# Four early weight halves held back until the last pair's scores, two loads begun ahead of the layers, two halves a step in the first block

## The chip, the cores and the metric

The kernel runs on one core of one Trainium2 chip. The metric is the device time of one launch in microseconds (us). Before the change three runs took 1002.86, 1002.90 and 1004.34 us, with a median of 1002.9 us.

## The reference

Inputs are q, k and v of shape (4, 8, 576, 64) and four weight matrices in fp32. What is computed, cut to its core:

```python
scores = scale * q @ k.T                       # per batch and head, 576 x 576
mask = block_i >= block_j                      # causal by blocks of 64
attn = exp(scores - max); attn = attn / (sum + 1e-9)
x = (attn @ v)                                 # -> 2304 tokens x 512
h = x @ w_in;  g = relu(h) ** 2;  x = g @ w_out      # layer 0, hidden width 2048
h = x @ w_in2; g = h * cos(h);    out = g @ w_out2   # layer 1
```

## The kernel before

**Attention.** Two heads of one batch form a pair, so there are 16 pairs. A pair has nine query blocks of 64. For each block i, TensorE (PE) multiplies the stacked queries of both heads with the keys up to block i (`scores`, L374). VectorE (DVE) takes the negated maximum (`nmax`, L386), ScalarE (ACT) the exponential with its sum (L391). GpSimd (POOL) adds the guard to the sums (L416), VectorE inverts them (`rinv`, L422) and GpSimd scales the probabilities P (L431). TensorE transposes P in 128 x 128 pieces, four to a PSUM bank, 25 to a pair (L452). ScalarE writes the high part of each bank (`PTh`, L457) and VectorE subtracts it for the low part (`PTl`, L460; the last, of 64 keys, is written into PTh). TensorE multiplies both parts with the split values `vhl` (L517), ScalarE moves one half of the result (`half`, L528) and VectorE joins the halves into `xall` (L531).

**The order in attention.** A planner (class `Plan`) sets it. Each operation is added with an engine, an estimated cost and a rank, which is a number of the table RANK plus ten times the pair. The planner gives each engine, again and again, the operation that can start first; among those that can start equally early the smallest rank wins. The result is one fixed list for each engine, which the chip runs in that order.

**The weights.** Each layer has 16 chunks of its hidden width, and each chunk has two weight halves, one of w_in (h = 0) and one of w_out (h = 1), 128 x 512 numbers stored as 64-bit words. A half is loaded (`raw`, L202, four buffers) and turned into a high and a low fp32r part by ten instructions: on VectorE `shift` (L205), `mask` (L212), `join` (L223), `sign` (L235), `power` (L241) and `low` (L265); on ScalarE `rebias` (L218) and `fraction` (L229); and `high`, which is on GpSimd (L259) while attention runs and on ScalarE (L256) in the layers. The halves are taken in the order in which the first block of tokens needs them: halves 0, 1 and 2 are w_in of chunks 0 to 2, half 3 is w_out of chunk 0, half 4 is w_in of chunk 3, then alternately w_out and w_in, up to half 28, which is w_in of chunk 15, and the last three of w_out. Layer 0 has halves 0 to 31.

EARLY halves, six of them, are put into the plan of attention. All others are turned by `convert()`, which the layers call. One call finishes the half that the call before it had begun, begins the next, and loads one more.

**The layers.** Tokens go through in blocks, 512 in the first. A step is one chunk of one block: `hidden` (12 matmuls, L614) makes h, ScalarE and VectorE make g and split it (`gs`: relu, square and the high part on ScalarE, the low part on VectorE, L629), and `output` (12 matmuls, L678) follows three steps later (LAG). The vector work of a chunk is issued one and two steps after its `hidden`. A table PACE says how many calls of `convert` follow each step: 1.67 in the first block, 2 in blocks that it does not name. When the last chunk of a block has been issued, the block after it is split into high and low parts (`Cut`: `xs`, L315 on ScalarE and L318 on VectorE), and the first `hidden` of the new block reads them. Halves of layer 1 wait until layer 0's buffers come free, in the last block of layer 0. Each engine runs its instructions in the order in which this code issues them. The first token block lies in batch 0, which pairs 0 to 3 make, so its `Cut` (four on ScalarE, four on VectorE) is part of the plan of attention.

Of the kernel before, what the change touches and what calls it, by code (L numbers as in the profile page):

```python
# [24 lines left out]


RANK = {
    "load": -165.7,
    "k scale": -157.7,
    "scores": 2.2,  # L30
    "maximum": -10.7,
    "exponential": -2.3,
    "guard": -163.0,
    "invert": -9.5,
    "scale": 29.9,
    "turn": 15.2,
    "turned high": -300.7,
    "turned low": 10.0,
    "value load": -108.7,
    "value high": 42.3,  # L40
    "value low": 41.1,
    "weighted": 21.0,
    "move": 20.5,
    "join": 18.3,
    "keep": 215.5,
    "add": 497.7,
    "zeros": -334.9,
    "weights": 136.7,
    "cut": 1000000.0,
}  # L50

# [79 lines left out]
def tile_block_causal_attention__then__two_ffn(  # L131
# [13 lines left out]
    NPAIR, _, S = kT.shape  # L145
    D = vp.shape[4]
# [23 lines left out]
    nc.vector.memset(new_bias, -7.0 * 2.0**30)  # L170

    WARM = 15
    EARLY = 6
    NA = 5
    w_a = ctx.enter_context(tc.tile_pool(name="w_a", bufs=NA))
    xs_p = ctx.enter_context(tc.tile_pool(name="xs", bufs=1))
# [8 lines left out]
    weights = {}  # L185
    LAG = 3
    loads = [((layer, c), h) for layer in range(2) for c in range(KF) for h in range(2)]
    loads.sort(key=lambda x: (x[0][0], x[0][1] + LAG * x[1], -x[1]))
    loads.reverse()
    loaded, begun = [], []  # L190
# [81 lines left out]
    def flush():  # L272
        while later:
            later.pop()()

    def convert():

        old = new = None
        flush()
        if begun:  # L280
            (layer, c), h = begun[0].key, begun[0].h
            if layer == 1 and c >= freed[h]:
                return
            old = begun.pop()
            old.sign()
        if loaded:
            new = loaded.pop()
            begun.append(new)
            new.shift()
        if old:  # L290
            old.power()
            old.high()
        if new:
            new.mask()
            new.rebias()
        if old:
            old.low()
        if new:
            new.join()
            later.append(new.fraction)  # L300
        if loads:
            loaded.append(Half(*loads.pop()))
            loaded[0].load()

    class Cut:

# [18 lines left out]
    def attention():  # L325
        with ExitStack() as actx:
            ap = actx.enter_context(tc.tile_pool(name="ap", bufs=1))
            ps = actx.enter_context(tc.tile_pool(name="ps", bufs=1, space=PSUM))
            plan = Plan([ps.tile([128, 512], F32, name=f"ps{r}") for r in range(6)])
# [170 lines left out]
            def add_weighted(p, e, i0, i1):  # L500

                rank = 10 * p + e + i0 / 20
                b, hp = divmod(p, KD)
                mine, other = slice(e * D, (e + 1) * D), slice((1 - e) * D, (2 - e) * D)
                pt = [t.rearrange("p (s e d) -> p s e d", e=2, d=D) for t in PT]
                todo = [
                    (j, max(i0, 2 * j), x)
                    for j in range(NCH)
                    if 2 * j < i1
                    for x in range(1 if j == NCH - 1 else 2)  # L510
                ]
                w, at = (i1 - i0) * D, slice(i0 * D, i1 * D)

                def product(bank):
                    for n, (j, a, x) in enumerate(todo):
                        s0 = j_off[j] + a - 2 * j
                        nc.tensor.matmul(  # L517
                            bank[:, (a - i0) * D : w],
                            lhsT=vhl[:, j, e].rearrange("p x d -> p (x d)"),
                            rhs=pt[x][:, s0 : s0 + i1 - a, e, :],  # L520
                            start=(n == 0),
                            stop=(n == len(todo) - 1),
                        )

                x = xall[mine, hp, b * S : (b + 1) * S][:, at]

                def move(bank):
                    nc.scalar.activation(out=half[e][mine, at], in_=bank[other, 0:w], func=AF.Copy)  # L528

                def join(bank):  # L530
                    nc.vector.tensor_tensor(out=x, in0=bank[mine, 0:w], in1=half[e][mine, at], op=ALU.add)  # L531

                need = sorted({n // 4 for n, (_, i) in enumerate(seq) if i0 <= i < i1})
                keys = [f"{x}{g}" for x in ("PTh", "PTl", "room") for g in need] + ["vh", "vl"]
                cost = sum(max(0.107, (i1 - a) * D / 2400 + 0.0135) for _, a, _ in todo)
                s = plan.add("P", cost, ("weighted", rank), product, keys, [f"O{p}.{e}.{i0}"], holds=1)
                product_, half_, x_ = f"O{p}.{e}.{i0}", f"half{e}.{i0}", f"x{b}.{hp}.{e}.{i0}"
                out_of = lambda f: lambda bank=None: f(plan.held[s][0])
                plan.add("A", 0.052 + w / 1200, ("move", rank), out_of(move), [product_], [half_])
                plan.add("V", 0.07 + w / 960, ("join", rank), join, [product_, half_], [x_], frees=s)  # L540

            def add_zeros(r):

# [7 lines left out]
            def add_half(n):  # L551
                x = Half(*loads.pop())
                raw, high, bits = f"raw{n % 4}", f"high{n % 4}", f"bits{n % 2}"
                rank = ("weights", n)
                plan.add("D", 2.0, rank, x.load, writes=[raw, high])
                plan.add("V", 0.34, rank, x.shift, writes=[raw])
                plan.add("V", 0.34, rank, x.mask, [high], [bits])
                plan.add("A", 0.61, rank, x.rebias, writes=[bits])
                plan.add("V", 0.6, rank, x.join, [high], [raw])
                plan.add("A", 0.52, rank, x.fraction, writes=[raw])  # L560
                plan.add("V", 0.6, rank, x.sign, [high], [bits])
                plan.add("V", 0.34, rank, x.power, [bits], [high])
                plan.add("G", 0.67, rank, x.high_beside, [bits])
                plan.add("V", 0.6, rank, x.low, [raw, high])
# [5 lines left out]
            for p in range(NPAIR):  # L570
                if p < 2:
                    add_zeros(p)
                add_loads(p)
                for i in range(NB):
                    add_scores(p, i)
                for g in range(len(groups)):
                    add_normalise(p, g)
                for g in range((len(seq) + 3) // 4):
                    add_transposes(p, g)
                add_values(p)  # L580
                for e in range(2):
                    for i0, i1 in ((0, 4), (4, NB)):
                        add_weighted(p, e, i0, i1)
            for n in range(EARLY):
                add_half(n)
            for kk in range(KD):
                x = Cut(0, S // 128 * 128, kk)
                keys = [f"x0.{kk}.{e}.{i0}" for e in range(2) for i0 in (0, 4)]
                plan.add("A", 0.52, ("cut", kk), x.high, keys, [f"xs{kk}"])
                plan.add("V", 0.6, ("cut", kk), x.low, [f"xs{kk}"])  # L590
                first.append(x)
# [3 lines left out]
    def layers():  # L595
# [112 lines left out]
                t0 += n  # L708
        last = max(i for i, b in enumerate(blocks) if b[0] == 0)
        steps = [(i, c) for i in range(len(blocks)) for c in range(KF)]  # L710
        PACE = {0: 1.67, last: 1.75, last + 1: 0.75}
        owed = 0.0
        gss = {}
        xs = first
# [1 line left out]
        for step in range(len(steps) + LAG):  # L716
# [4 lines left out]
            if step < len(steps):  # L721
                i, c = steps[step]
                layer, t0, n = blocks[i]
                while (layer, c, 0) not in weights:
                    convert()
                gss[step], *fresh = hidden(layer, c, xs, n)
# [10 lines left out]
            if step < len(steps) and i == last:  # L737
                freed[0] = c + 1
            owed += PACE.get(i, 2)
            while owed >= 1:  # L740
                owed -= 1
                convert()
            if step >= LAG:
                i, c = steps[step - LAG]
                layer, t0, n = blocks[i]
                while (layer, c, 1) not in weights:
                    convert()
                output(layer, gss.pop(step - LAG), n, c)
                if i == last:
                    freed[1] = c + 1  # L750
                if c == KF - 1:
                    finish(layer, t0, n)

    with tc.manual_schedule():
        attention()
        layers()
# [43 lines left out]
```

## Time and profile before

| | us |
|---|---|
| median of three runs | 1002.9 |
| time of the profiled execution | 1003.09 |
| its span, first to last instruction | 1001.3 |
| TensorE busy | 981.8 (98%) |
| VectorE busy | 644.4 (64%) |
| ScalarE busy | 580.5 (58%) |
| GpSimd busy | 146.1 (15%) |
| first matmul of the layers starts | 202.96 |

TensorE is nearly always busy when the whole span is taken together. That is an average over stages: GpSimd works in attention alone (up to about 200 us), and VectorE is nearly full in attention and in the first block of layer 0 (up to about 282 us), while TensorE runs without a gap after that. The granted TensorE clock of the whole run was 0.998 of 2.4 GHz.

### The profile page before, as it was taken

What the parts mean: (1) busy time and instruction counts of PE and PEld (TensorE: products, weight loads), DVE (VectorE), ACT (ScalarE), POOL (GpSimd) and SP (SyncE); (2) the same over time, 40 slices, a digit from 0 to 9 for tenths busy, and PEclk for the clock granted to TensorE, in tenths of its full rate; (3) what the DMA queues carried; (4) which work ended last, traced back from release to release, by engine and by line L of the source; (5) the groups of instructions that cost most, each with busy time, mean ns of one, the idle gap of its engine ahead of it and who ended that gap; (6) DMA issues with size and microseconds to landing.
All of it is one profiled execution on the core that took longest, in us unless ns stands there. A gap on an engine that the chain in (4) does not pass through costs nothing.

```text
span 1001.3 us, 13718 instructions
## 1 busy us (share of the span) xinstructions
PE 981.8 (98%) x4895; PEld 823.2 (82%) x4895; DVE 644.4 (64%) x1292; ACT 580.5 (58%) x1192; POOL 146.1 (15%) x260
## 2 busy tenths in 40 slices
PE   8899999999999999999999999999999999999998
PEld 7677777888778889988888888888888888899996
DVE  5999999889972121211169999966555655656554
ACT  6898888878874343443368886644334434434433
POOL 6577777700000000000000000000000000000000
PEclk9999999999999999999999999999999999999999
DMA  6442332225430000000014442001000100100000
GB/s 224 139 141 98 98 99 99 98 87 169 166 125 1 1 1 1 1 1 1 1 63 139 163 141 85 1 1 42 1 1 1 43 1 1 43 1 1 32 1 31
DMA packets 18803, 58.54 MB, mean 58 GB/s; under 512 B 1968, under 2 KB 2096, under 8 KB 18736
## 3 DMA queue, kind: packets, MB, share of 16 engines
q1 hardware_dynamic: 18736, 57.68, 17.1%
q8 instruction: 38, 0.62, 0.3%
q14 instruction: 29, 0.24, 0.1%
HBM read 52.95 MB, written 4.72 MB: 58 GB/s over the span
## 4 chain that ended last, share of the span: by engine, by line
PE 78%; DVE 17%; ACT 2%; issue 1%; DMA 1%; POOLq 0%; POOL 0%; SPq 0%; ACTq 0%; DVEq 0%
PE acc L678 36%; PE h L614 36%; DVE nmax L386 3%; DVE PTl L460 3%; PE ps L374 2%; PE ps L517 2%; DVE w L265 2%; DVE raw L223 2%; DVE xall L531 2%; DVE bits L235 2%; PE ps L452 2%; DVE raw L205 1%; DVE raw L241 1%; DVE gs L629 1%; ACT P L391 1%
## 5 line engine op out<-in xcount | busy, mean ns | idle before, releaser
L614 PE MATMUL h<-xs,w 128*128 128x512 f32 (+2 forms) x1920 | 422.1, 369 | 1.8 <-ACT w L256 1.3
L614 PEld LDWEIGHTS h<-xs,w 128*128 128x128 f32 x1920 | 344.1, 188 | 59.6 <-ACT w L256 3.4
L678 PE MATMUL acc<-gs,w 128*128 128x512 f32 (+1 forms) x960 | 210.2, 368 | 0.0
L678 PE MATMUL acc<-w,gs 128*128 128x512 f32 x864 | 209.7, 391 | 0.0
L678 PEld LDWEIGHTS acc<-gs,w 128*128 128x128 f32 x960 | 168.4, 189 | 29.9
L629 DVE TENSOR_TENSOR gs<-g,gs 128x512 fp32r<-128x512 f32 (+2 forms) x160 | 101.4, 634 | 141.6 <-ACT gs L626 141.5
L678 PEld LDWEIGHTS acc<-w,gs 128*128 128x128 f32 x864 | 161.8, 188 | 32.1
L626 ACT CAST gs<-g 128x512 fp32r<-128x512 f32 (+2 forms) x160 | 92.3, 577 | 150.0 <-DVE g L661 96.7
L647 DVE SCALAR_TENSOR_TENSOR g<-turns,h 128x512 f32<-128x512 int32 (+1 forms) x80 | 50.7, 634 | 123.0 <-ACT turns L644 122.2
L374 PE MATMUL ps<-kB,qB 128*128 128x64 f32 (+7 forms) x256 | 83.9, 427 | 4.4 <-DVE PTl L460 1.6
L644 ACT ACTIVATE turns<-h 128x512 int32<-128x512 f32 (+1 forms) x80 | 44.2, 552 | 70.5 <-PE h L614 70.4
L636 ACT ACTIVATE g<-h 128x512 f32<-128x512 f32 (+1 forms) x80 | 43.8, 548 | 66.7 <-PE h L614 65.9
L431 POOL TENSOR_SCALAR P<-P,rinv 128x64 f32<-128x64 f32 (+2 forms) x144 | 78.0, 556 | 29.0 <-DVE rinv L422 27.0
L391 ACT ACTIVATE P<-ps,nmax 128x64 f32<-128x64 f32 (+7 forms) x128 | 64.1, 503 | 24.1 <-DVE nmax L386 19.4
L658 ACT ACTIVATE g<-g,half_pi 128x512 f32<-128x512 f32 (+1 forms) x80 | 54.6, 682 | 36.9 <-DVE g L652 36.9
L452 PEld LDWEIGHTS ps<-ident,P 128*128 128x128 f32 (+1 forms) x400 | 47.3, 141 | 34.4 <-DVE PTl L460 14.0
L452 PE MATMUL ps<-ident,P 128*128 128x128 f32 (+1 forms) x400 | 62.7, 279 | 6.4 <-DVE xall L531 2.4
L460 DVE TENSOR_TENSOR PTl<-ps,PTh 128x512 fp32r<-128x512 f32 x96 | 63.7, 677 | 1.6 <-ACT PTh L457 1.2
L386 DVE TENSOR_REDUCE nmax<-ps 128x1 f32<-128x64 f32 (+7 forms) x128 | 56.4, 449 | 7.9 <-PE ps L374 6.8
L517 PE MATMUL ps<-PTh,vhl 128*128 128x320 f32 (+3 forms) x224 | 60.0, 301 | 0.9 <-DVE PTl L460 0.5
L457 ACT CAST PTh<-ps 128x512 fp32r<-128x512 f32 (+1 forms) x112 | 58.1, 541 | 1.6 <-PE ps L452 1.0
L218 ACT ACTIVATE bits<-bits,new_bias 128x512 int32<-128x512 int32 x64 | 46.4, 725 | 12.6 <-DVE bits L212 12.5
(50 smaller groups left out, 944.9 us busy)
## 6 DMA issues: line engine op xcount, KB each, us to landing
raw<-in_w_dram SPq DMA_DIRECT2D x64, 512.0 KB, 3.7
qB<-in_qd_dram SPq DMA_DIRECT2D x15, 576.0 KB, 3.9
v_raw<-in_vp_dram SPq DMA_DIRECT2D x16, 320.0 KB, 2.9
kB<-in_kT_dram SPq DMA_DIRECT2D x16, 288.0 KB, 2.8
out_dram<-o SPq DMA_DIRECT2D x8, 512.0 KB, 3.9
out_dram<-o SPq DMA_DIRECT2D x2, 256.0 KB, 2.9
qB<-in_qd_dram SPq DMA_DIRECT2D x1, 384.0 KB, 5.2
qB<-in_qd_dram SPq DMA_DIRECT2D x1, 192.0 KB, 2.8
```

Source lines behind the costliest of these rows:

```text
L374: nc.tensor.matmul(bank[:, 0:w] if one else wide[:, x, 0:w], lhsT=qB[r][:, i].rearrange("p e d -> p (e d)"), rhs=kB[r][:, x * w : (x + 1) ...
L386: nc.vector.tensor_reduce(out=nmax[i], in_=held(), axis=AX.X if one else AX.XY, op=ALU.max, negate=True)
L391: nc.scalar.activation(out=mine if one else mine.rearrange("p (x w) -> p x w", x=2), in_=held(), func=AF.Exp, bias=nmax[i], scale=1.0, acc ...
L431: nc.gpsimd.tensor_scalar(out=mine, in0=mine, scalar1=inverse[:, i - i0 : i - i0 + 1], scalar2=1.0, op0=ALU.mult, op1=ALU.mult,)
L452: nc.tensor.transpose(bank[0:keys, n * 128 : (n + 1) * 128], P[r][:, o : o + keys], ident)
L457: nc.scalar.copy(out=PT[0][0:keys, at], in_=plan.held[s][0][0:keys, 0:w])
L460: nc.vector.tensor_tensor(out=PT[1][:, at] if keys == 128 else PT[0][keys:128, at], in0=bank[0:keys, 0:w], in1=PT[0][0:keys, at].bitcast(F32),
L517: nc.tensor.matmul(bank[:, (a - i0) * D : w], lhsT=vhl[:, j, e].rearrange("p x d -> p (x d)"), rhs=pt[x][:, s0 : s0 + i1 - a, e, :], start ...
L614: nc.tensor.matmul(h, lhsT=w[:, a, kk * 128 : (kk + 1) * 128], rhs=xs[kk].parts[:, x], start=(m == 0), stop=(m == 3 * KD - 1),)
L626: nc.scalar.copy(out=gs[:, 0], in_=g)
L629: nc.vector.tensor_tensor(out=gs[:, 1], in0=g, in1=gs[:, 0].bitcast(F32), op=ALU.subtract)
L678: nc.tensor.matmul(dst, lhsT=lhsT, rhs=rhs, start=(c == 0 and m == 0), stop=(c == KF - 1 and m == 2),)
```

## The change

The table RANK gets new numbers (two of its lines stand here for all). Four halves in place of six are put into attention's plan, and their `shift` and `mask` now also depend on the first scores of the last pair. The loads of the next two halves are issued from attention's plan, and `convert` takes halves from a list that holds two loaded ones. In the first block two calls of `convert` follow each step. Two cost estimates of the planner change.

```diff
 RANK = {
-    "exponential": -2.3,
+    "exponential": 485.3,
...
-    "weights": 136.7,
+    "weights": 181.2,
...
-    EARLY = 6
+    EARLY = 4
...
         if loaded:
-            new = loaded.pop()
+            new = loaded.pop(0)
...
             loaded.append(Half(*loads.pop()))
-            loaded[0].load()
+            loaded[-1].load()
...
-                plan.add("A", 0.052 + w / 1200, ("move", rank), out_of(move), [product_], [half_])
-                plan.add("V", 0.07 + w / 960, ("join", rank), join, [product_, half_], [x_], frees=s)
+                plan.add("A", 0.19 + w / 1200, ("move", rank), out_of(move), [product_], [half_])
+                plan.add("V", 0.07 + 0.12 * e + w / 960, ("join", rank), join, [product_, half_], [x_], frees=s)
...
                 rank = ("weights", n)
+                late = f"S{NPAIR - 1}.0"
                 plan.add("D", 2.0, rank, x.load, writes=[raw, high])
-                plan.add("V", 0.34, rank, x.shift, writes=[raw])
-                plan.add("V", 0.34, rank, x.mask, [high], [bits])
+                plan.add("V", 0.34, rank, x.shift, [late], [raw])
+                plan.add("V", 0.34, rank, x.mask, [high, late], [bits])
...
             for n in range(EARLY):
                 add_half(n)
+            for n in range(EARLY, EARLY + 2):
+                x = Half(*loads.pop())
+                loaded.append(x)
+                plan.add("D", 2.0, ("weights", n), x.load, writes=[f"raw{n % 4}", f"high{n % 4}"])
...
-        PACE = {0: 1.67, last: 1.75, last + 1: 0.75}
+        PACE = {0: 2, last: 1.75, last + 1: 0.75}
```

**VectorE where attention ends.** `xall` rows are joins, `PTl` and `PTh` rows the low parts of the last pair's transposed probabilities (the `PTh` row is the last of them), `raw`, `bits` and `w_` rows belong to weight halves. Before the change, no half stands among the last pair's rows, and half 6 begins behind the last joins:

```order
L531 TENSOR_TENSOR xall<-ps_84,half_118 64x320
L460 TENSOR_TENSOR PTl<-ps_88,PTh 128x512
L460 TENSOR_TENSOR PTl<-ps_86,PTh 128x512
L460 TENSOR_TENSOR PTl<-ps_83,PTh 128x512
L460 TENSOR_TENSOR PTl<-ps_87,PTh 128x512
L460 TENSOR_TENSOR PTl<-ps_85,PTh 128x512
L460 TENSOR_TENSOR PTh<-ps_84,PTh 64x128
L531 TENSOR_TENSOR xall<-ps_88,half_117 64x256
L531 TENSOR_TENSOR xall<-ps_86,half_118 64x256
L531 TENSOR_TENSOR xall<-ps_83,half_117 64x320
L531 TENSOR_TENSOR xall<-ps_87,half_118 64x320
L205 TENSOR_SCALAR raw<-raw 128x512
```

After the change, in the same place, halves 0 and 1 stand ahead of the last five `PTl` rows (`w_1968` is half 0), and halves 1 to 3 follow the `PTh` row:

```order
L460 TENSOR_TENSOR PTl<-ps_87,PTh 128x512
L241 TENSOR_SCALAR raw<-bits 128x512
L212 TENSOR_SCALAR bits<-raw 128x512
L265 TENSOR_TENSOR w_1968<-raw 128x512
L531 TENSOR_TENSOR xall<-ps_86,half_117 64x320
L223 SCALAR_TENSOR_TENSOR raw<-raw 128x512
L531 TENSOR_TENSOR xall<-ps_85,half_118 64x320
L460 TENSOR_TENSOR PTl<-ps_88,PTh 128x512
L460 TENSOR_TENSOR PTl<-ps_83,PTh 128x512
L460 TENSOR_TENSOR PTl<-ps_84,PTh 128x512
L460 TENSOR_TENSOR PTl<-ps_87,PTh 128x512
L460 TENSOR_TENSOR PTl<-ps_86,PTh 128x512
```

Nine instructions of halves now stand between the first joins of the pair before the last and the `PTh` row: two each of shift, mask and join, and one each of sign, power and low. From the `PTh` row on, sign, power and low of half 1 and everything of halves 2 and 3 are to come, and only then half 4.

**VectorE where the second block begins.** `gs` rows are the low parts of g, `xs` rows the cuts of the second block. Before, the cuts stand behind the low part of chunk 13; `w_2907` is half 28, and what is left of half 29 and the halves 30 and 31 follow the cuts:

```order
L265 TENSOR_TENSOR w_2907<-raw 128x512
L223 SCALAR_TENSOR_TENSOR raw<-raw 128x512
L629 TENSOR_TENSOR gs<-g,gs 128x512
L318 TENSOR_TENSOR xs_2947<-xall,xs_2947 128x512
L318 TENSOR_TENSOR xs_2950<-xall,xs_2950 128x512
L318 TENSOR_TENSOR xs_2953<-xall,xs_2953 128x512
L318 TENSOR_TENSOR xs_2956<-xall,xs_2956 128x512
L235 SCALAR_TENSOR_TENSOR bits<-raw,bits 128x512
L205 TENSOR_SCALAR raw<-raw 128x512
```

After, the same cuts again follow the low part of chunk 13, but `w_2948` ahead of them is half 31, the last of layer 0:

```order
L212 TENSOR_SCALAR bits<-raw 128x512
L265 TENSOR_TENSOR w_2948<-raw 128x512
L223 SCALAR_TENSOR_TENSOR raw<-raw 128x512
L634 TENSOR_TENSOR gs<-g,gs 128x512
L318 TENSOR_TENSOR xs_2988<-xall,xs_2988 128x512
L318 TENSOR_TENSOR xs_2991<-xall,xs_2991 128x512
L318 TENSOR_TENSOR xs_2994<-xall,xs_2994 128x512
L318 TENSOR_TENSOR xs_2997<-xall,xs_2997 128x512
L634 TENSOR_TENSOR gs<-g,gs 128x512 x3
```

Counted from the `PTh` row to the low part of chunk 13, VectorE's list holds 31 instructions of each of the six kinds of a half, 14 low parts of gs and four joins after the change. Before, it held 23 of sign, power and low, 24 of shift, mask and join, 14 low parts and four joins.

## Rows read from the trace of the kernel before

**Rows 1.** The page, part 1: busy time, share of the span and instructions of each engine.
```profile
PE 981.8 (98%) x4895; PEld 823.2 (82%) x4895; DVE 644.4 (64%) x1292; ACT 580.5 (58%) x1192; POOL 146.1 (15%) x260
```

**Rows 2.** The chain of waits, 185 to 300 us: start us, us, what ran.
```profile
207.80 0.73 ACT bits L218
208.55 0.69 DVE bits L235
...
280.64 2.56 PE h L614 x10
...
285.93 2.72 PE h L614 x12
```

**Rows 3.** Busy time by stretch: us, then busy us of each engine (instructions), clock, DMA.
```profile
175.21:186.31 11.10, 11.10 (x73) 9.20 (x71) 9.73 (x24) 10.02 (x32) 8.38 (x16) 1.00 0.59 196
...
36.11:175.21 139.10, 129.82 (x784) 102.06 (x783) 135.65 (x292) 118.20 (x334) 103.61 (x171) 0.99 0.33 106
```

**Rows 4.** Busy time by stretch, VectorE alone, in the first block.
```profile
208.55:281.70 73.15, 73.15 (x152) 1.00 0.48 159
```

**Rows 5.** Timeline, all engines, second block's begin: start us, us, engine, instruction.
```profile
281.86 0.65 ACT L229 ACTIVATE raw<-raw 128x512 f32<-128x512 uint32 x1
...
285.76 2.88 PE L614 MATMUL h<-xs,w 128*128 128x512 f32 x12
```

**Rows 6.** Timeline of TensorE: first transposes of pairs, first layer.
```profile
24.49 0.66 PE L452 MATMUL ps<-ident,P 128*128 128x128 f32 x4
...
36.11 0.66 PE L452 MATMUL ps<-ident,P 128*128 128x128 f32 x4
...
175.21 0.60 PE L452 MATMUL ps<-ident,P 128*128 128x128 f32 x4
...
186.31 0.66 PE L452 MATMUL ps<-ident,P 128*128 128x128 f32 x4
...
202.96 9.32 PE L614 MATMUL h<-xs,w 128*128 128x512 f32 x40
```

**Rows 7.** Timeline of VectorE; in brackets the idle time before and its releaser.
```profile
38.18 1.75 DVE L212 TENSOR_SCALAR bits<-raw 128x512 int32<-128x512 int32 x1
...
186.90 1.01 DVE L531 TENSOR_TENSOR xall<-ps,half 64x320 f32<-64x320 f32 x2 [1.26 <-ACT half L528]
...
201.12 0.28 DVE L460 TENSOR_TENSOR PTh<-ps,PTh 64x128 fp32r<-64x128 f32 x1
...
280.50 0.69 DVE L223 SCALAR_TENSOR_TENSOR raw<-raw 128x512 int32<-128x512 int32 x1
...
281.10 0.69 DVE L629 TENSOR_TENSOR gs<-g,gs 128x512 fp32r<-128x512 f32 x1
...
283.57 2.50 DVE L318 TENSOR_TENSOR xs<-xall,xs 128x512 fp32r<-128x512 f32 x4 [1.78 <-ACT xs L315]
```

**Rows 8.** Groups of VectorE, 0 to 203 us: count | busy us, mean ns | idle before.
```profile
L531 DVE TENSOR_TENSOR xall<-ps,half 64x256 f32<-64x256 f32 (+1 forms) x63 | 28.5, 453 | 5.2 <-ACT half L528 3.5
...
L223 DVE SCALAR_TENSOR_TENSOR raw<-raw 128x512 int32<-128x512 int32 x6 | 6.1, 1014 | 0.1
...
L205 DVE TENSOR_SCALAR raw<-raw 128x512 int32<-128x512 int32 x6 | 5.0, 834 | 0.0
...
L235 DVE SCALAR_TENSOR_TENSOR bits<-raw,bits 128x512 int32<-128x512 int32 x6 | 4.8, 795 | 0.1
...
L212 DVE TENSOR_SCALAR bits<-raw 128x512 int32<-128x512 int32 x6 | 4.3, 721 | 0.0
...
L265 DVE TENSOR_TENSOR w<-raw 128x512 fp32r<-128x512 f32 x6 | 4.2, 706 | 0.1
...
L241 DVE TENSOR_SCALAR raw<-bits 128x512 int32<-128x512 int32 x6 | 3.5, 577 | 0.1
```

**Rows 9.** Groups of GpSimd, 0 to 203 us.
```profile
L259 POOL TENSOR_SCALAR w<-bits 128x512 fp32r<-128x512 f32 x6 | 3.9, 648 | 3.4 <-DVE bits L235 3.4
```

**Rows 10.** Timeline of GpSimd.
```profile
38.06 1.58 POOL L492 TENSOR_TENSOR vhl<-v_raw,vhl 128x640 fp32r<-128x640 f32 x1
```

More of the change, by code (lines that the diff above doesn't have):

```diff
@@ L27 @@
 RANK = {
[L28 to L31, printed above, removed]
-    "exponential": -2.3,
[L33 to L47, printed above, removed]
-    "weights": 136.7,
+    "load": -388.7,
+    "k scale": -506.7,
+    "scores": 0.2,
+    "maximum": -16.0,
+    "exponential": 485.3,
+    "guard": -148.0,
+    "invert": -12.1,
+    "scale": -145.6,
+    "turn": 13.1,
+    "turned high": -90.7,
+    "turned low": -1.1,
+    "value load": -78.8,
+    "value high": -109.4,
+    "value low": 28.0,
+    "weighted": 21.6,
+    "move": 1000,
+    "join": 34.2,
+    "keep": 67.5,
+    "add": 125.4,
+    "zeros": -32.1,
+    "weights": 181.2,
     "cut": 1000000.0,
```

## The prediction, made before the changed kernel had run

> **What bounds the kernel now.** I read the page's busy shares first. They show TensorE at 98% [rows 1], which hides that two stages have another bound; the chain of waits shows this. From 208.55 to 280.64 us the chain runs through VectorE, half after half. Ahead of that stands one wait for ScalarE's rebias at 207.80, and behind it TensorE alone up to the end [rows 2]. The table by stretches shows the other stage. From the first transposes of pair 2 to those of pair 13 VectorE is busy for 135.65 of 139.10 us. In the stretch of pair 13, where no half and no cut is left, it is busy for 9.73 of 11.10, and TensorE for the full 11.10 [rows 3]. So VectorE bounds a pair that carries pieces of halves, and TensorE bounds a pair that carries none. In the first block VectorE is busy for all of 73.15 us with 152 instructions [rows 4]. The change shifts VectorE's work from the first stage to the second, and the question is which loses more.
>
> Everything behind the first `hidden` of the second block is TensorE alone, and the change leaves it as it is. So I work out when this `hidden` starts, which was at 285.76 [rows 5]. All sums are against the profiled execution (span 1001.3, time 1003.09); the median is 0.2 us lower.
>
> **Attention up to the last two pairs: -16.5 us.** The transposes that open a pair's turn started at 36.11 for pair 2 and at 186.31 for pair 14 [rows 6], which is 150.2 us for 12 pairs. After the change no half stands there, and the lists of a pair look like those of pair 13. At 11.10 us a pair, the 12 take 133.2, which is 17.0 less. It cannot be less than 11.10, since TensorE is full there. The four low parts of the first cut still sit in four of these pairs. I give them 0.5 in all, because VectorE has 1.37 us to spare in a pair. The other end is 11.62 us a pair, as between 24.49 and 36.11 [rows 6], a turn without halves too; it would leave a gain of 10.8. I take 11.10, since pair 13 is the nearest row, and keep both ends. The new ranks are not priced by themselves: where TensorE has no gap, the order of the others is covered by it.
>
> **The last two pairs: +4.0 us.** The end of VectorE's `PTh` row (201.40 before [rows 7]) closes attention. Nine instructions of halves now stand ahead of it, one and a half halves. At their durations in attention, with 0.08 us less for each since neighbours overlap, they take 2 x 0.834 + 2 x 0.721 + 2 x 1.014 + 0.795 + 0.577 + 0.706 - 0.7 = 6.5 us [rows 8]; at those of the first block 1.5 x 2.81 = 4.2 (2.81 is worked out below). VectorE's spare time is 1.37 in 11.10 us, so about 2.0 over the 16 us of the tail; the wait of 1.26 at 186.90 is part of it [rows 7]. So the delay is 2.2 to 4.5, or 6.5 where nothing hides it. I take 4.0, nearer to attention's durations, since GpSimd works there until the end. GpSimd's high part of half 0 is part of this. It waits for VectorE's sign, and behind it in GpSimd's queue stand the guard and all scales of the last pair, for which the transposes wait.
>
> So the `PTh` row ends at 201.40 - 16.5 + 4.0 = 188.9.
>
> **From there to the low part of chunk 13: +17.0 us.** A row of 0.69 us holds VectorE for 0.60 (280.50 to 281.10 [rows 7]). Of the 152 instructions in 73.15 us, 14 are low parts of gs of that length, so the other 138 (23 halves) take (73.15 - 8.4) / 138 = 0.469 each, which is 2.81 a half. After the change 31 x 6 = 186 such instructions, 14 low parts and four joins (0.45 each [rows 8]) lie between the `PTh` row and the end of chunk 13's low part: 87.2 + 8.4 + 1.8 = 97.4 us. Before, it was 281.79 - 201.40 = 80.4. The work grows by 7.5 halves, 21.1 us: four and a half were done in attention before, and three stood behind this place. The two loads begun ahead give 4.2 back, because 80.4 held that much waiting (80.4 - 23.5 x 2.81 - 8.4 - 1.8). Their place in SyncE's queue costs nothing, since only further halves stand behind them. ScalarE's two more high parts lie beside VectorE, which is the fuller of the two.
>
> **GpSimd beside it: +0.8 us.** The high parts of halves 1 to 3 (648 ns each [rows 9]) run on GpSimd after the `PTh` row, beside VectorE's half instructions. VectorE's mask at 38.18 took 1.75 us while GpSimd's subtraction ran from 38.06 to 39.64 [rows 7, 10], so a blocked instruction waits about as long as GpSimd's lasts: at most 3 x 0.65 = 1.9. At least it is 0, since the low parts of halves took 706 ns in attention, as good as free of it [rows 8]. I take 0.8, between the two. The Trainium skill (SBUF — State Buffer, "Who interferes with whom") says that a VectorE instruction with two SBUF inputs contends with a GpSimd instruction that reads SBUF, and that the second to issue fully blocks. By that rule the term would be 1.9 and the sum 4.3; by the rows of the low parts, which have two SBUF inputs and do not show it, 0 and 2.4.
>
> **Into the second block: -2.1 us.** The low part of chunk 13 ended at 281.79, and `hidden` started 4.0 later. Now it waits for the first cut. ScalarE's fraction started at 281.86 [rows 5] and the first cut's low part at 283.57 [rows 7], 1.71 apart, and this is the same sequence now. The fraction can start some 0.2 after the last join, which ends 0.6 ahead of the low part's end. That puts the cut's low part 1.3 behind the low part of chunk 13, and with its 0.69 and one matmul (0.23) that runs ahead of it, `hidden` 1.9 behind it.
>
> Sum: -16.5 + 4.0 + 17.0 + 0.8 - 2.1 = +3.2. `hidden` starts at 289.0 instead of 285.76. The time is 1003.09 + 3.2 = 1006.3, and against the median 1006.1.
>
> **What covers what.** TensorE alone would reach the second block after 29 groups of 2.72 us from 202.96 [rows 2, 6], at 281.8, that is 80.4 behind the `PTh` row; after the change this would be 269.3. So TensorE will stand idle for about 20 us in all in the first block. It waits first for half 4 (chunk 3): its low part is VectorE's 27th instruction behind the `PTh` row, 23 x 0.469 + 1.8 = 12.6 us on, and TensorE asks for it 1.56 + 3 x 2.72 = 9.7 on, so about 3 us early. Then it loses 0.8 us a step, since two halves and one low part take 6.2 and a step 5.44. A lower clock after such a wait would cost nothing while TensorE is this far ahead.
>
> **The rivals.**
> - *The tail hides its halves.* The last pairs wait in turn for ScalarE, GpSimd and TensorE, and the halves fall into VectorE's gaps. Then the tail costs 2 or less, the cuts and GpSimd nothing: -17.0 + 2.0 + 17.0 - 2.1 = -0.1, so 1002.8; with a tail of 0.5 it is 1001.3. For it: VectorE's waits there. Against it: the rows of halves stand ahead of the five `PTl` rows on the same engine. It decides from a tail of 3 us downward. Chance 0.26.
> - *The pairs do not reach TensorE's pace.* At 11.62 a pair the gain shrinks by 6.2 and the time is 1012.3. For it: that interval, and ScalarE at 10.02 of 11.10 in pair 13 [rows 3]. Against it: pair 13 itself. Chance 0.17.
> - *Three steps of lag swallow the halves.* If the first block were bound by TensorE, which two halves a step are to keep supplied, `hidden` would start at 269.3 and the time be 986.4. Against it: 73.15 of 73.15 [rows 4], and at least as many halves as before. Chance 0.05.
>
> **How the numbers follow.** The forecast (1004 to 1009) has a chance of 0.50, the rivals 0.26, 0.17 and 0.05, and 0.02 is left. What a measurement can tell from no change is 0.2%, 2 us. Slower by more: 0.46 of the forecast, all of the second rival and 0.02 of the rest, 0.65. Within it: 0.18 of the first rival and 0.04 of the forecast, 0.22. Faster: 0.08 of the first rival and the third, 0.13. The range for 8 in 10 is 1001.5 to 1011: it takes in most of the first rival and the nearer part of the second.
>
> **What would show it.** In the profile after, the transposes of pair 14 start near 170 (at 176 the second rival holds); the `PTh` row ends near 189; VectorE has no gap from there to the first cut of the second block, about 99 us; chunk 3's `hidden` waits about 3 us; and the first `hidden` of the second block starts near 289. If VectorE has gaps in the first block while TensorE has none, the third rival is right. The forecast is wrong if that `hidden` starts before 287.8.

## The result and the profile after

The changed kernel takes 1007.96 us in the median (1007.44 to 1010.53, four runs), and the kernel before, run beside it, 1002.88 (1001.93 to 1004.34, four runs). The ratio is 1.0054 with an interval of 1.0033 to 1.0076, so the change costs about 5 us. The forecast was 1006.1, in a range from 1001.5 to 1011. The profiled execution of the changed kernel has a span of 1006.3 and a time of 1008.09 us.

The page's first part, to be laid beside [rows 1]:

```profile
PE 981.6 (98%) x4895; PEld 826.7 (82%) x4895; DVE 638.2 (63%) x1292; ACT 585.1 (58%) x1194; POOL 142.1 (14%) x258
```

It tells nothing of the 5 us: TensorE is busy for the same 98%. The stages tell it. The busy time by stretch, from the first transposes of pair 2, which come at 35.04 here, to those of pair 14, with the columns of [rows 3]:

```profile
35.04:167.28 132.24, 132.24 (x855) 110.89 (x854) 121.30 (x282) 123.01 (x352) 99.38 (x180) 1.00 0.32 108
```

TensorE (the first busy number) now has no gap in these pairs, and VectorE (the third) is the one with room: the bound of the stage has changed sides. The timeline of TensorE, for [rows 6] and the border in [rows 5]: pair 14's first transposes, three waits in the last two pairs, the layers' first matmuls, the begin of the second block, and the first `output` of layer 1.

```profile
167.28 0.66 PE L452 MATMUL ps<-ident,P 128*128 128x128 f32 x4
...
170.72 0.91 PE L374 MATMUL ps<-kB,qB 128*128 128x384 f32 x2 [0.94 <-ACT P L391]
...
182.33 1.64 PE L452 MATMUL ps<-ident,P 128*128 128x128 f32 x13 [1.30 <-POOL P L431]
184.66 0.39 PE L517 MATMUL ps<-PTh,vhl 128*128 128x256 f32 x1 [0.69 <-POOL vhl L492]
...
193.49 13.19 PE L619 MATMUL h<-xs,w 128*128 128x512 f32 x48 [5.29 <-DVE xall L531]
...
287.02 5.79 PE L619 MATMUL h<-xs,w 128*128 128x512 f32 x12 [3.04 <-ACT xs L315]
292.61 3.28 PE L683 MATMUL acc<-gs,w 128*128 128x512 f32 x12
295.72 2.88 PE L619 MATMUL h<-xs,w 128*128 128x512 f32 x12
...
617.18 3.01 PE L683 MATMUL acc<-w,gs 128*128 128x512 f32 x12 [0.36 <-ACT xall L696]
```

Pair 14 opens 19.0 us earlier than before; 1.0 of this is there at pair 0's first transposes already (11.93 against 12.92). Then two waits stand out that were not there before: 5.29 us ahead of the layers and 3.04 us ahead of the second block, where twelve matmuls take 5.79 us in place of 2.88. The timeline of VectorE, for [rows 7]: two instructions of half 0 in the tail, the last `PTh` row, one instruction beside GpSimd, the low part of chunk 13 and the cuts.

```profile
178.75 0.65 DVE L241 TENSOR_SCALAR raw<-bits 128x512 int32<-128x512 int32 x1
179.64 1.10 DVE L265 TENSOR_TENSOR w<-raw 128x512 fp32r<-128x512 f32 x1
...
185.56 0.28 DVE L460 TENSOR_TENSOR PTh<-ps,PTh 64x128 fp32r<-64x128 f32 x1
...
186.82 0.85 DVE L241 TENSOR_SCALAR raw<-bits 128x512 int32<-128x512 int32 x1
...
283.86 0.70 DVE L634 TENSOR_TENSOR gs<-g,gs 128x512 fp32r<-128x512 f32 x1
287.00 2.50 DVE L318 TENSOR_TENSOR xs<-xall,xs 128x512 fp32r<-128x512 f32 x4 [2.44 <-ACT xs L315]
```

The busy time of VectorE alone from 189.83 to that low part, for [rows 4] (columns: busy, clock, DMA share, GB/s):

```profile
189.83:284.55 94.72, 94.24 (x197) 0.96 0.48 167
```

It idles for 0.5 us in 94.7. What it took on is simply done there. The granted clock around the second block's begin, two us a row (after the busy times of PE, PEld, DVE, ACT and POOL, the clock as a share of 2.4 GHz):

```profile
286.00:288.00 2.00, 0.98 (x2) 0.54 (x3) 1.00 (x2) 2.00 (x5) 0.00 (x0) 0.64 0.09 35
288.00:290.00 2.00, 2.00 (x5) 1.59 (x6) 2.00 (x4) 1.94 (x5) 0.00 (x0) 0.50 0.00 0
290.00:292.00 2.00, 2.00 (x6) 1.58 (x5) 0.79 (x2) 0.34 (x1) 0.00 (x0) 0.50 0.00 0
292.00:294.00 2.00, 2.00 (x7) 1.58 (x7) 0.00 (x0) 1.12 (x2) 0.00 (x0) 0.65 0.00 0
294.00:296.00 2.00, 2.00 (x11) 1.63 (x10) 0.00 (x0) 0.13 (x2) 0.00 (x0) 1.00 0.00 0
```

After the wait of 3.04 us TensorE got 1.2 GHz (0.50) until about 293: five or six matmuls in 2 us in place of eleven. From the second block's first `hidden` to the next one passed 8.70 us, against 5.44 before (285.76 to 291.20). So 1.26 us of the loss arise before that `hidden` and 3.26 between it and the next one. The 4.52 stand unchanged up to layer 1's first `output`, which waits for ScalarE and starts at 617.18, 5.04 us later than before (612.14). This is the rest of the span's 5.0; why ScalarE comes later there stays open.

### The profile page after: what moved, and what is told of

It is laid out like the page before. It is cut to its first block, busy times and chain, and to the rows that moved or that the text cites. A ratio compares the mean times of both kernels' runs of the same rounds, so it can differ in the third digit from the quotient of the medians.

```text
span 1006.3 us, 13883 instructions
## 1 busy us (share of the span) xinstructions
PE 981.6 (98%) x4895; PEld 826.7 (82%) x4895; DVE 638.2 (63%) x1292; ACT 585.1 (58%) x1194; POOL 142.1 (14%) x258
## 3 DMA queue, kind: packets, MB, share of 16 engines
q1 hardware_dynamic: 18736, 57.68, 16.5%
## 4 chain that ended last, share of the span: by engine, by line
PE 75%; DVE 18%; ACT 3%; issue 2%; POOL 1%; DVEq 0%; ACTq 0%; POOLq 0%
PE acc L683 32%; PE h L619 31%; PE ps L374 4%; PE ps L517 3%; DVE bits L235 3%; DVE w L265 3%; PE ps L452 3%; DVE raw L223 3%; DVE raw L205 2%; DVE raw L241 2%; DVE gs L634 1%; DVE PTl L460 1%; PE wide L374 1%; DVE nmax L386 1%; POOL P L431 1%
## 5 line engine op out<-in xcount | busy, mean ns | idle before, releaser
L619 PEld LDWEIGHTS h<-xs,w 128*128 128x128 f32 x1920 | 347.7, 190 | 65.4 <-ACT raw L229 5.4
L683 PE MATMUL acc<-gs,w 128*128 128x512 f32 (+1 forms) x960 | 214.3, 370 | 5.6 <-DVE gs L634 5.6
L452 PE MATMUL ps<-ident,P 128*128 128x128 f32 (+1 forms) x400 | 59.4, 275 | 2.0 <-POOL P L431 1.9
```

The source lines that it names most:

```text
L452: nc.tensor.transpose(bank[0:keys, n * 128 : (n + 1) * 128], P[r][:, o : o + keys], ident)
L619: nc.tensor.matmul(h, lhsT=w[:, a, kk * 128 : (kk + 1) * 128], rhs=xs[kk].parts[:, x], start=(m == 0), stop=(m == 3 * KD - 1),)
L683: nc.tensor.matmul(dst, lhsT=lhsT, rhs=rhs, start=(c == 0 and m == 0), stop=(c == KF - 1 and m == 2),)
```

## The experiments

Theory A is the prediction's: VectorE's work up to the second block's first `hidden` sets the time, and TensorE only follows. All ratios are to the kernel before in the same series of runs (medians 1001.92, 1001.96 and 1002.43 us). Places in two traces can differ by 1 us and more without any change: pair 0's first transposes came at 11.93, 11.75 and 12.76 us in three executions with one and the same plan of attention, and at 12.92 and 14.52 in two with the plan of before.

**Only the pace put back.**

```diff
-        PACE = {0: 2, last: 1.75, last + 1: 0.75}
+        PACE = {0: 1.67, last: 1.75, last + 1: 0.75}
```

Expected: 

> The changed kernel with the first block's pace back at 1.67; all else as changed. Theory A (two halves a step put halves 29 to 31 ahead of the second block's cuts, and a lower clock follows the wait for them): from the end of the last PTh row, 185.84 in the changed kernel, 28 halves instead of 31 stand ahead of the cuts, 185.84 + 28 x 2.81 + 8.4 + 1.8 + 0.4 = 275.1 for chunk 13's low part; then half 28 decides, and the first hidden of the second block starts near 279 instead of 287.0, at full clock: 8 us plus the 3 us of the slow matmuls, 11 in all, so about 997, under both kernels. Rival B (the halves have to be done anyway; those put behind the cuts make the outputs of chunks 13 to 15 wait instead): within 2 us of the changed kernel, 1006 to 1010.

Measured: 999.80 us, ratio 0.9976 (0.9967 to 0.9985), 8.2 us less than the changed kernel (7.8 by the two ratios). Theory A holds in sign and nearly in size. The second block's `hidden` starts at 282.07 and not at 279. The 3 us arise ahead of the cut: chunk 13's low part ended at 278.12 and not at 275.1, with VectorE losing 1.66 us to ScalarE in one place. The cut itself waited 1.77 us, as it did before (1.78 [rows 7]). VectorE's timeline:

```profile
200.18 0.70 DVE L265 TENSOR_TENSOR w<-raw 128x512 fp32r<-128x512 f32 x1 [1.66 <-ACT raw L229]
...
279.89 2.50 DVE L318 TENSOR_TENSOR xs<-xall,xs 128x512 fp32r<-128x512 f32 x4 [1.77 <-ACT xs L315]
```

**Only the pace changed.** The kernel before with `PACE = {0: 2, ...}`.

Expected: 

> The kernel before with the pace of two halves a step alone. Theory A: the rest of half 29 and halves 30 and 31 move ahead of the cuts, three more halves (8.4 us) on a VectorE that is full; half 6 starts some 2 us earlier, because its rebias is issued ahead of the first chunk's relu; the first hidden of the second block starts 3 to 5 us later than 285.76, and where TensorE then waits about 3 us the clock costs 3 more: 1006 to 1011. Rival B (the place of the last halves does not matter): 1003 or below, since the stalls of 3.9 us in the first block go.

Measured: 1009.07 us, ratio 1.0075 (1.0063 to 1.0088). The pace alone costs 7 us in the old order, against 8 in the new one, and the rest of the change gives 1 to 2. With two halves a step all 32 halves are turned ahead of the second block's cut; with 1.67 only 29 and a half are, counted in VectorE's list. The time is in A's range, but A's lower clock is not in the profiled execution, the slowest of the five (1011.35 us). There TensorE waits 0.77 us for the cuts and keeps its clock:

```profile
292.27 0.51 PE L614 MATMUL h<-xs,w 128*128 128x512 f32 x1 [0.77 <-ACT xs L315]
293.00 2.81 PE L614 MATMUL h<-xs,w 128*128 128x512 f32 x11 [0.22 <-DVE xs L318]
...
298.36 2.88 PE L614 MATMUL h<-xs,w 128*128 128x512 f32 x12
```

This `hidden` starts 6.5 us later than before; 1.6 of them are there at pair 0 already (14.52 against 12.92).

**The clock at the second block.** Thirteen matmuls whose result nobody reads stand ahead of the second block's first `hidden`, in the changed kernel:

```diff
+            if layer == 0 and c == 0 and len(gss) > 1:
+                fill = weights[0, KF - 1, 0]
+                for _ in range(13 if hb[0] == KF + 1 else 0):
+                    nc.tensor.matmul(
+                        h, lhsT=fill[:, 0, 0:128], rhs=fill[:, 0, 0:n], start=True, stop=True,
+                    )
```

Expected: 

> The changed kernel with 13 extra matmuls on TensorE (2.9 us at full clock, their result overwritten) between the last output of the first block's twelfth chunk and the second block's first hidden, where TensorE waits 3.04 us for the cuts. Theory A (that wait lowers the clock, and the first hidden then takes 5.6 us instead of 2.72 and the output behind it 3.1): with the wait filled both take 2.72, the time falls by about 3.2 us, to 1004.8. Rival C (the first hidden is slow because the cuts come one after the other, 0.6 us each, and not because of the clock): no gain, 1008.

Measured: 1005.88 us, ratio 1.0038 (1.0025 to 1.0051), 2.1 us less than the changed kernel, or 1.6 by the two ratios, whose intervals overlap; so the rows have to show the effect. TensorE's timeline, and the busy times around the last pair's matmuls with the clock behind them:

```profile
285.17 3.11 PE L619 MATMUL h<-w 128*128 128x512 f32 x13
288.37 0.50 PE L625 MATMUL h<-xs,w 128*128 128x512 f32 x1
289.09 2.82 PE L625 MATMUL h<-xs,w 128*128 128x512 f32 x11 [0.23 <-DVE xs L318]
...
294.47 2.88 PE L625 MATMUL h<-xs,w 128*128 128x512 f32 x12
...
185.00:187.00 2.00, 2.00 (x12) 1.82 (x10) 1.65 (x4) 1.71 (x5) 0.39 (x1) 0.50 0.00 0
```

The same twelve matmuls run at full clock now, and from one `hidden` to the next it is 6.10 us in place of 8.70. So it is the idle time, and not anything in these matmuls, that brought the lower clock, and it cost 2.6 us. The 6.10 are still 0.66 more than the 5.44 of before: the cuts come one after the other and the first matmuls wait for them, as with the pace alone, where it is 6.09 at full clock. To that extent Rival C holds too. In this profile attention ended 1.3 us later, which takes away part of what the clock gave back. Of that, 0.8 is there from pair 0 on (12.76 against 11.93); the rest comes with a clock of 0.50 from 185 to 187, where the changed kernel had 1.00.

**Without the loads begun ahead.** The kernel with the pace put back, less the lines that issue two loads from attention's plan:

```diff
-            for n in range(EARLY, EARLY + 2):
-                x = Half(*loads.pop())
-                loaded.append(x)
-                plan.add("D", 2.0, ("weights", n), x.load, writes=[f"raw{n % 4}", f"high{n % 4}"])
```

Expected: 

> As the run with the pace back at 1.67, and without the two loads begun ahead: the layers begin with nothing loaded, as before the change. Theory A (the loads ahead give back VectorE's waits at the first block's start, 4.2 us in the kernel before): 3 to 4 us above the run with the pace back alone. Rival D (VectorE has halves 1 to 3 and four joins to do there anyway, and the loads are in time without being ahead): within 1 us of it.

Measured: 1001.50 us, ratio 0.9994 (0.9985 to 1.0002), 1.7 more than with them, between the two expectations. VectorE's timeline shows the wait that they remove, but with them 1.66 and 0.35 us of other waits for ScalarE take half of its place:

```profile
200.90 0.69 DVE L235 SCALAR_TENSOR_TENSOR bits<-raw,bits 128x512 int32<-128x512 int32 x1 [4.34 <-ACT bits L218]
```

**The last joins first.** The kernel with the pace put back and `"weights": 300` in place of 181.2. It tests the wait of 5.29 us ahead of the layers, which the prediction had missed.

Expected: 

> Change: the changed kernel with 1.67 halves a step and the rank of the halves raised from 181.2 to 300, so that the last joins of the last pair stand ahead of halves 2 and 3 on VectorE. Theory A (VectorE is the bound up to the second block, and only what it does or waits for there counts): the first hidden of the layers starts at about 188 instead of 193.3 and keeps the full clock, but of the end only the waits of VectorE for ScalarE in the first steps (0.16 + 1.66 + 0.35 us with 1.67 halves a step alone) can go: 997 to 999 us, against 999.8. Theory E (the TensorE stop of 5.3 us with the half clock behind it is itself on the path): 5.3 + 2.2 us earlier, 992 to 994.

Measured: 998.18 us, ratio 0.9960 (0.9946 to 0.9974): the lowest median of all. TensorE's timeline:

```profile
189.70 8.45 PE L619 MATMUL h<-xs,w 128*128 128x512 f32 x36 [1.14 <-DVE xall L531]
200.77 4.61 PE L619 MATMUL h<-xs,w 128*128 128x512 f32 x12 [2.62 <-ACT w L256]
...
281.44 2.88 PE L619 MATMUL h<-xs,w 128*128 128x512 f32 x12
```

TensorE starts 3.6 us earlier in the layers and waits 2.62 us for a weight instead, with the lower clock behind it. The second block's `hidden` comes only 0.63 us earlier than at 282.07. So the wait ahead of the layers was covered: Theory A, not E, though the clock that A kept full fell here too.

**The old ranks.** The kernel with the pace put back and the old RANK table.

Expected: 

> Change: the changed kernel with 1.67 halves a step and the table RANK of the kernel before (late halves, four of them, and the two loads stay). The plan then has the four halves between the scores of the last pair and its last transposes, and three of the four are done before the last PTh row. Theory A (what left the middle of attention is the gain, the ranks only place it): pair 14's first transposes come at 167 to 168 again, the tail is 27 to 30 us in place of 18.6 as it holds some 2.5 halves (4.6 us each) more, and 2.5 x 2.81 us fewer follow: 1001 to 1005 us. Theory F (the new ranks themselves speed up the middle pairs): pair 14's first transposes come at 175 or later, 1006 or more.

Measured: 1008.40 us, ratio 1.0066 (1.0053 to 1.0079). The time is F's, but not its reason: from pair 4's `PTh` row to pair 13's they came 11.07 to 11.10 us apart, no slower than A takes them. The last `PTh` rows of pairs 13 and 15:

```profile
166.79 0.28 DVE L460 TENSOR_TENSOR PTh<-ps,PTh 64x128 fp32r<-64x128 f32 x1
...
201.05 0.28 DVE L460 TENSOR_TENSOR PTh<-ps,PTh 64x128 fp32r<-64x128 f32 x1
```

Up to pair 13 it is as fast as A says: that row stood at 183.21 before, so 16.4 us came from the halves that left the middle, old ranks or not. (In the changed kernel it stands at 163.99, so the new ranks add 2.8, of which 2.2 arise in pairs 2 to 4.) Then the plan puts all four halves ahead of and between the maxima of the last pair's first three blocks (175.86, 181.30 and 182.97), and what the middle gained is lost, as busy time by stretch shows:

```profile
170.00:175.00 5.00, 0.00 (x0) 0.00 (x0) 5.00 (x10) 1.94 (x4) 1.98 (x2) 0.73 0.09 29
```

VectorE works on halves alone and TensorE on nothing. A had these halves run beside the pairs; they ran in their place.

**Not held back.** The kernel with the pace put back, `shift` and `mask` without `late`.

Expected: 

> Change: the changed kernel with 1.67 halves a step, its shift and mask no longer tied to the last pair's scores: the four halves lie among pairs 2 to 9 again. Theory A: VectorE has 4 x 4.65 = 18.6 us more in the middle, of which some 8 us fit into its gaps; pair 14's first transposes at 175 to 179 (167.1 when late), the tail back at 15, the last PTh row at about 192, and 2.9 halves x 2.81 = 8 us less behind it: 998 to 1001 us, so that holding them back is worth nothing or little by itself. Theory G (holding back is the gain): 1005 or more.

Measured: 1000.52 us, ratio 0.9981 (0.9972 to 0.9990), 0.7 more than when held back, which the intervals do not part. The opening of pair 14 and the last `PTh` row:

```profile
180.06 0.66 PE L452 MATMUL ps<-ident,P 128*128 128x128 f32 x4
...
194.79 0.28 DVE L460 TENSOR_TENSOR PTh<-ps,PTh 64x128 fp32r<-64x128 f32 x1
```

The second block's `hidden` starts at 283.67, against 282.07. Pair 14 opens at 180.06 and the `PTh` row starts at 194.79, each later than A said (175 to 179, 192). The four halves cost 9.4 us up to the `PTh` row and save 7.8 to the `hidden`. Holding back is worth little by itself.

**The ranks alone.** The kernel before with the new RANK table.

Expected: 

> Change: the kernel before with the new table RANK alone (six halves among pairs 1 to 11, 1.67 halves a step). Theory A: VectorE's work is unchanged, attention stays bound by it: 1000 to 1004 us, pair 14's first transposes at 184 to 188. Theory F (the new ranks speed up the pairs): pair 14's first transposes at 180 or earlier, 996 or less.

Measured: 999.83 us, ratio 0.9978 (0.9967 to 0.9988), just ahead of what A allowed and far from F. Pair 14 opens at 182.78, 3.5 us earlier than before (1.2 of them at pair 0, 11.72 against 12.92), and the second block's `hidden` starts at 282.05, 3.7 earlier. So the ranks alone give as much as all of the change without its pace. The old wait for rebias is still there, 3.06 us at 204.82.

**Six and eight halves among the pairs.** The kernel that doesn't hold them back, with `EARLY = 6` and `EARLY = 8`.

Expected with six: 

> Change: the kernel of the run without late halves, with six early halves in place of four (so against the new ranks alone it adds only the two loads begun ahead and the two cost estimates). Theory A: the pairs go as with the new ranks alone (last PTh row at about 197.5), the wait of 3.06 us of the first half behind the last joins shrinks to some 0.5 us, the second block's first hidden comes 2.5 us earlier than with the new ranks alone (279.5): 997 to 998 us. Rival H (the wait is only moved to ScalarE or a weight behind): 999 to 1000.5, as with the new ranks alone (999.8).

Expected with eight: 

> Change: as the run with six early halves and the two loads begun ahead, with eight early halves. Theory A: two halves more among the pairs are 2 x 4.65 = 9.3 us of VectorE there, of which some 4 us fit where it idles beside the last five pairs; two fewer of 2.81 us follow, so the second block's first hidden moves by 9.3 - 4 - 5.6 = -0.3 us against six: 996.5 to 998.5. Rival I (the pairs are bound by VectorE to the end, nothing fits): 1001 or more.

Measured: 1002.26 us (ratio 0.9997, 0.9989 to 1.0006) and 1008.94 (1.0057, 1.0043 to 1.0070). Theory A failed both times, and H with it. With eight the time is Rival I's, but not its reason: two halves more delayed pair 14 by 4.9 us (190.71 against 185.78), so about half of their 9.3 us did fit, as A took it. TensorE's timeline at the second block with six:

```profile
284.45 0.49 PE L618 MATMUL h<-xs,w 128*128 128x512 f32 x1 [0.45 <-ACT xs L315]
```

and with eight, with the busy times from the layers' first matmul to there:

```profile
207.92:289.50 81.58, 79.17 (x350) 65.25 (x349) 78.11 (x163) 70.34 (x122) 0.00 (x0) 1.00 0.47 155
...
289.50 0.51 PE L618 MATMUL h<-xs,w 128*128 128x512 f32 x1 [2.42 <-ACT xs L315]
```

I had taken it that a half done in attention is one fewer in the first block. It is not where the pace is ahead of the need: then the number of steps decides how many calls of `convert` stand ahead of the cut. VectorE's list has 25 halves (24 for three of the six kinds) between the `PTh` row and the cut with six and with eight alike, one more than with the ranks alone. With eight, TensorE has no gap in the first block but for the 2.42 us at its end, so every us by which attention ends later is lost, and the clock behind the 2.42 us takes 1.6 more (7.70 us to the next `hidden` in place of 6.11 with six). That with six the pairs also ran 3.0 us behind those of the ranks alone (pair 14 at 185.78) stays open: the two cost estimates and the loads differ, and I did not part them.

## Why the prediction was right, and where it was not

The mechanism held: VectorE's work moved from a stage that it bounds to another, and the second one loses more. The sum did not hold as well as the time. At the second block's `hidden` it was +3.2 us, and the trace shows +1.26, at 287.02. That is ahead of 287.8, which the prediction itself had named as the sign of being wrong. Behind that place about 3.8 us arise where the prediction had nothing. So it was 1.9 us too high there and 3.8 too low behind it, and 1006.1 missed 1007.96 by 1.9; that the two errors have opposite signs is luck.

| step | forecast | measured | from |
|---|---|---|---|
| attention up to pair 14 | -16.5 | -19.0 | 167.28 - 186.31 |
| the last two pairs | +4.0 | +3.5 | (185.84 - 167.28) - (201.40 - 186.31) |
| to the low part of chunk 13, with GpSimd | +17.8 | +18.3 | (284.56 - 185.84) - 80.4 |
| into the second block | -2.1 | -1.5 | (287.02 - 284.56) - 3.97 |
| that `hidden` waits for cut after cut | none | +0.7 | 6.10 - 5.44 |
| clock behind that `hidden` | none | +2.6 | 8.70 - 6.10 |
| layer 1's first `output` | none | +0.5 | (617.18 - 612.14) - 4.52 |

**Attention.** The step was right in kind and 2.5 us too small. 1.0 of this is there at pair 0 and can be the spread between executions. The pairs took 11.02 us each (132.24 / 12), so the sentence that it cannot be less than 11.10 was wrong, though TensorE was full in both; this is another 1.0. The 0.5 for the first cut's low parts was not needed. With the old ranks the halves' leaving gave 16.4 at pair 13, which is near the forecast. The new ranks, which I had held to be covered, add 2.8 to it; by themselves, with six halves in the pairs, they give 2.3 from pair 0 on.

**The tail.** Held: the halves are not hidden, 3.5 us for one and a half. The run that does not hold them back confirms it: with the same ranks and no half there, its tail takes 15.0 us (180.06 to 195.07), against 15.1 before and 18.6 after the change. The size came out by other rows than taken: the nine rows of halves last 0.41 to 1.10 us and 6.1 together, where 7.2 were taken. TensorE's waits there name ScalarE's and GpSimd's probabilities (0.94, 0.60 and 1.30 us); on which path the halves delay those stays open.

**The first block.** Held best: 98.7 us against 98.2, VectorE without a gap but for 0.5. Inside it, GpSimd cost VectorE one stretched instruction (0.85 against 0.42 us), 0.4 in place of 0.8. That it is VectorE's work that counts here is shown by the pace put back and by the pace alone.

**The border.** I let the cut's low part follow the fraction by 1.71 us. ScalarE's timeline shows why it was 3.0:

```profile
283.99 0.67 ACT L229 ACTIVATE raw<-raw 128x512 f32<-128x512 uint32 x1 [0.47 <-DVE raw L223]
284.56 0.58 ACT L641 ACTIVATE g<-h 128x512 f32<-128x512 f32 x1
285.17 0.63 ACT L642 ACTIVATE g<-g 128x512 f32<-128x512 f32 x1
285.83 0.62 ACT L631 CAST gs<-g 128x512 fp32r<-128x512 f32 x1
286.36 2.17 ACT L315 CAST xs<-xall 128x512 fp32r<-128x512 f32 x4
```

The fraction now waits for the last half's join, and relu, square and high part of the next chunk stand behind it in ScalarE's list, ahead of the cut.

**The clock.** The failed step is that everything behind the second block's first `hidden` is left as it is, together with the sentence that a lower clock would cost nothing while TensorE is this far ahead. The sentence holds for the wait that it spoke of. Behind that wait VectorE works without a gap but for 0.5 us, and in the run with the last joins first, where TensorE waits 1.14 and 2.62 us in place of 5.3 and the low clock comes later, the second block moved by 0.63 us. It does not hold at the border, where I had TensorE idle as well and did not ask what follows. From there on TensorE is the bound, so all of the 3.3 us to the next `hidden` count. The run with the thirteen matmuls shows that 2.6 of them are the clock and 0.7 the cuts. The Trainium skill (TensorE: Matmul & The Clock Gate, Part 1) would have led me to look: it tells of a clock that falls when TensorE idles, and the trace agrees, with 0.50 behind the wait of 3.04 us.

**The waiting ahead of the layers.** I forecast that TensorE starts 1.56 us behind the `PTh` row, as before, and then waits 3 us for chunk 3's half. It started 7.65 us behind (193.49 - 185.84), since the last joins stand behind halves on VectorE, and then ran 48 matmuls in one piece. This cost next to nothing.

**The rivals.** The first one decides from a tail of 3 us downward, and the tail was 3.5. The second needed 11.62 us a pair; the pairs took 11.02. The third needed gaps on VectorE in the first block, and there is 0.5 us in 94.7.

## What to carry to other kernels

When work moves from one stage to another, count from the instruction lists how much of it stands ahead of the instruction at which the bound changes; a pace in the code, and not the number of pieces done earlier, may fix that count. Price the parts of a change apart: here the new order alone gave 2 us and the pace alone cost 7. Where TensorE is the bound from some point on and must first wait at that point, add what its clock takes to come back: 2.6 us behind a wait of 3.04 here. Before a difference between two traces is put down to a change, see how far executions of one list lie apart.

## What the runs showed that was not expected

One of GpSimd's high parts beside a gapless VectorE was itself held up. It takes 0.65 us in attention [rows 9] and took 3.21 in the changed kernel's timeline of GpSimd:

```profile
190.21 3.21 POOL L259 TENSOR_SCALAR w<-bits 128x512 fp32r<-128x512 f32 x1 [2.82 <-DVE bits L235]
```

It lasted to 193.42, while VectorE's instructions from 189.46 to 192.27 followed each other without a gap and kept their durations (0.41 and 0.67 to 0.68 us). It ended in the middle of the two rows that follow, a join of 0.47 us that reads PSUM and a power. The prediction had let VectorE pay. VectorE did pay beside the high part ahead of this one (0.72 us from 186.66), in the row of 0.85. Spans on GpSimd are rough, but the same row took 3.21 us in three more executions that have this order on VectorE (pace put back, thirteen matmuls, no loads ahead). With the last joins first the order differs, and there the high part took 0.73 and VectorE's power beside it 0.85. What decides between the two is not shown.

A TensorE wait ahead of the layers of 5.29 us was followed by a granted clock of 0.50 as well, and waits of 2.62 us (last joins first) and 2.42 us (eight halves) by twelve matmuls in 4.61 us and eleven in 4.29. After 0.45 and 0.23 us at the second block's begin with six halves, the next eleven matmuls took 2.82 us as ever. One and the same list does not always bring the same clock: the wait of 1.30 us in the last pair was followed by 1.00 in the changed kernel, and one of 1.31 us, in the run with the thirteen matmuls, by 0.65 and then 0.50.
